# Spatial weights cast ahead of the last w_in quarter and of w_out, in an attention and gated-MLP kernel

## The chip, the cores and the metric

One NeuronCore of a Trainium2 chip. The metric is device time in microseconds (us) of one execution. Runs are timed beside runs of the kernel before on the same chip; a run over 1.5% above the fastest of its kernel is called slow and left out. A ratio in this document is the mean time of one kernel's fast runs over the mean of the other's fast runs of the same rounds, so it is not quite the ratio of the medians that stand beside it.

## The reference

Attention with grouped heads (8 batches, 16 query heads on 4 key heads, 384 positions, head size 64), whose output goes through a gated MLP with a mix over positions:

```
x     = attention(q, k, v)                    # [8, 384, 1024]
h     = max(x @ w_in, 0); u, v = halves of h  # w_in 1024 x 1024
v_n   = layernorm(v)
v_s   = w_spatial @ v_n + b_spatial           # 384 x 384, over positions
out   = (u * v_s) @ w_out                     # w_out 512 x 1024
```

Inputs and output are f32; the kernel computes in f16 with f32 sums.

## The kernel before

Work is written as words in strings, played in order; the program of each engine holds its own words in that order. `s`, `e`, `x`, `V`, `p`, `U`, `O` are scores, exponentials, values, and the MLP's parts; a plus means the next batch. The words that matter:

```python
# lk lq lv: load k, q, v of a batch on SP;  ck cq cv: cast them on GpSimd
# tk tq:    transpose k, q by DMA on SP
# wv wu:    load a quarter of w_in with a cast during the DMA, issued by GpSimd
# wo:       the same for w_out;  ws: load spatial weights and bias on SP
# cws: three casts of the spatial weights and a copy of the bias, on GpSimd
# tws: transpose them by DMA, issued by SP
RAMP1 = """
    ...
    cv wu0 lk+ lq0+ lq1+ lv+ ws ck+ cq0+ wv1
    ...
    cq1+ wu1 cv+ wo cws
    m10 r10 s16 e16 H0 x100 n100 x101 n101 s17 e17 s0+ e0+
    H1 s1+ e1+ m11 r11 s2+ e2+ x110 n110 x111 n111 Q10+ tws"""
FIRST = """lk+ lq0+ lv+ lq1+          # batch 2's loads, behind tws on SP
    s3 e3 s4 e4 V0' S0' s5 e5 V1' S1' ck+ cq0+
    s6 e6 s7 e7 V2' S2' s8 e8 Q11 tk+ tq0+ cq1+ cv+
    ...
    s15 s16 s17 e15 e16 e17 p2' U2' p3' U3' a10 a11"""

def cast_ws(engine):
    for tt in range(NST):
        engine.tensor_copy(ws16[:, tt, :, :],
            ws32[:, tt, :].rearrange("p (s t) -> p t s", t=NST))
    engine.tensor_copy(bias_tp..., bias_raw...)      # cut
```

SP sends its DMAs in the order of its program (in the first trace of before `tws` from 34.39 us, k from 37.11, q from 38.19), so batch 2's loads wait for `tws`, and `tws` waits for `cws` (13.2 us there). Batch 2's first scores on PE need its k and q, loaded, cast on GpSimd and transposed by DMA.

The softmax here doesn't subtract the row's maximum and nothing guards it: scores larger than these inputs give would overflow.

## Time and profile before

| | |
|---|---|
| time, median of the 3 runs first given | 253.27 us (253.07 to 253.46) |
| the profiled run | 256.59 us, its span on the core 254.8 us |
| PE, VectorE, ScalarE, GpSimd busy | 94%, 73%, 68%, 22% |

A busy share is an average over the span. Here PE is nearly full from batch 2 on (busy 90% or more in each of the page's 40 slices from 57.3 us to the last but one).

### The profile page before, as it was taken

How to read it: one execution, taken by the hardware profiler on the slowest of the kernel's cores; microseconds unless marked ns; L12 is line 12 of the kernel's file. 1: busy time of each engine (PE TensorE's matmuls, PEld its weight loads, DVE VectorE, ACT ScalarE, POOL GpSimd, SP SyncE). 2: the span in 40 equal slices, each digit the busy share in tenths (PEclk: the TensorE clock that was granted, in tenths of full speed). 3: DMA queues.
4: the chain of work that ended last, by engine and by line, in shares of the span. 5: the costliest groups of instructions: out<-in, count | busy, mean ns of one | idle time of the engine just before them, and what ended most of it. 6: DMA issues, size and time to landing. Idle time of an engine off the chain costs nothing.

```text
span 254.8 us, 6122 instructions
## 1 busy us (share of the span) xinstructions
PE 240.1 (94%) x2544; PEld 118.0 (46%) x2544; DVE 186.4 (73%) x347; ACT 172.1 (68%) x229; POOL 56.4 (22%) x100
## 2 busy tenths in 40 slices
PE   7689988859999999999999999999999999999993
PEld 6234434424355534444355444454355444554671
DVE  2536389985897679776996769776987669777853
ACT  3997999859596778678686778677785877430100
POOL 1825940552604400071004400170000000000000
PEclk9999999999999999999999999999999999999998
DMA  6999999989999383977099444958090202110324
GB/s 195 245 252 320 142 154 227 272 136 300 208 266 305 127 120 101 284 217 178 0 229 303 157 91 122 315 164 171 8 229 0 85 0 102 68 64 21 142 105 168
DMA packets 57228, 41.98 MB, mean 165 GB/s; under 512 B 26352, under 2 KB 53360, under 8 KB 57200
## 3 DMA queue, kind: packets, MB, share of 16 engines
q1 hardware_dynamic: 53936, 38.12, 56.9%
q0 software_dynamic: 2848, 3.15, 8.3%
q8 instruction: 20, 0.33, 0.5%
q10 hardware_dynamic: 416, 0.33, 0.4%
q14 instruction: 8, 0.07, 0.1%
HBM read 25.95 MB, written 12.58 MB: 151 GB/s over the span
## 4 chain that ended last, share of the span: by engine, by line
PE 57%; DVE 15%; DMA 13%; POOL 5%; issue 4%; ACT 3%; SPq 2%
PE banks L121 43%; DMA q<-in_q_dram 10%; PE banks L337 7%; PE banks L315 7%; DVE xT L407 3%; DVE sT L350 3%; DVE osb L545 3%; DVE v_n L481 3%; ACT aT L327 2%; POOL q L238 2%; POOL w_in L148 2%; DMA qT<-q 2%; DVE bn L467 1%; DVE v_r L454 1%; SPq L177 1%
## 5 line engine op out<-in xcount | busy, mean ns | idle before, releaser
L327 ACT ACTIVATE aT<-banks 128x1024 f16<-128x1024 f32 x144 | 136.6, 1025 | 38.2 <-PE banks L315 38.2
L315 PE MATMUL banks<-qT,kT 64*128 64x512 f16 x288 | 44.7, 380 | 6.8 <-DMA qT<-q 3.3
L121 PE MATMUL banks<-xT,w_in 128*128 128x384 f16 (+1 forms) x320 | 47.2, 294 | 0.8 <-DVE v_r L456 0.8
L121 PE MATMUL banks<-w_out,gT 128*32 128x512 f16 (+2 forms) x496 | 45.6, 378 | 0.0
L121 PE MATMUL banks<-w_in,xT 128*128 128x512 f16 x192 | 44.7, 380 | 0.1
L545 DVE COPY osb<-banks 128x512 f32<-128x512 f32 x46 | 30.4, 685 | 10.4 <-PE banks L121 10.4
L407 DVE TENSOR_TENSOR xT<-banks,rec 128x384 f16<-128x384 f32 x64 | 31.4, 550 | 8.9 <-ACT rec L376 8.8
L238 POOL CAST q<-q 128x384 f16<-128x384 f32 x57 | 30.5, 566 | 21.6 <-DMA q<-in_q_dram 19.9
L121 PEld LDWEIGHTS <-w_in 128*128 128x128 f16 x320 | 27.3, 98 | 16.2 <-issue 1.7
L337 PE MATMUL banks<-aT,v 128*32 128x384 f16 x768 | 34.4, 326 | 0.0
L121 PEld LDWEIGHTS <-gT 128*32 128x32 f16 (+1 forms) x496 | 18.7, 96 | 24.8 <-issue 6.4
L350 DVE TENSOR_TENSOR sT<-aT 128x1024 f16<-128x1024 f16 x39 | 30.1, 788 | 0.0
L121 PEld LDWEIGHTS <-xT 128*128 128x128 f16 x192 | 17.3, 98 | 25.4 <-issue 7.2
L195 POOL CAST k<-k 128x768 f16<-128x768 f32 x7 | 5.8, 829 | 93.0 <-DMA k<-in_k_dram 75.0
L315 PEld LDWEIGHTS <-kT 64*128 64x128 f16 x288 | 11.3, 94 | 31.5 <-issue 25.0
L337 PEld LDWEIGHTS <-v 128*32 128x32 f16 x768 | 20.6, 97 | 11.0 <-issue 1.2
L454 DVE TENSOR_SCALAR v_r<-banks 128x512 f32<-128x512 f32 x21 | 14.5, 692 | 13.4 <-PE banks L121 12.6
L525 DVE SCALAR_TENSOR_TENSOR gT<-banks,vs 128x384 f16<-128x384 f32 x24 | 13.4, 558 | 12.7 <-PE banks L121 12.2
L374 ACT ACTIVATE rec<-banks 128x384 f32<-128x384 f32 x32 | 15.7, 491 | 9.0 <-PE banks L337 9.0
L121 PE MATMUL banks<-wsT,v_n 128*128 128x384 f16 x96 | 20.6, 326 | 0.6
L376 ACT ACTIVATE rec<-rec 128x384 f32<-128x384 f32 x32 | 16.8, 524 | 1.0
L467 DVE BATCH_NORM_STATS2 bn<-v_r 128x6 f32<-128x512 f32 x24 | 16.7, 695 | 0.8
(49 smaller groups left out, 139.3 us busy)
## 6 DMA issues: line engine op xcount, KB each, us to landing
q<-in_q_dram SPq DMA_DIRECT2D x31, 384.0 KB, 7.1
out_dram<-osb SPq DMA_DIRECT2D x22, 512.0 KB, 3.1
v<-in_v_dram SPq DMA_DIRECT2D x8, 384.0 KB, 6.8
k<-in_k_dram SPq DMA_DIRECT2D x7, 384.0 KB, 5.5
w_in<-in_moe_w_in_dram POOLq DMA_DIRECT2D x16, 128.0 KB, 5.8
w_out<-in_moe_w_out_dram POOLq DMA_DIRECT2D x2, 512.0 KB, 9.1
out_dram<-osb SPq DMA_DIRECT2D x3, 256.0 KB, 2.0
ws<-in_moe_w_spatial_dram SPq DMA_DIRECT2D x1, 576.0 KB, 9.4
```

What stands on the lines that cost most here:

```text
L121: nc.tensor.matmul(dst[c : c + cols], w[:, c : c + cols], m, start=(i == 0), stop=(i == n - 1))
L238: engine(T["q16", b, gp][:, 2 * qd : 2 * qd + 2, :, half, :], T["q32", b, gp][:, qd, 2 * half : 2 * half + 2, :].rearrange("p j (t d) -> p ...
L315: nc.tensor.matmul(banks[:, xs[half], :], T["kT", b][lo:hi, t, gp, :], rhs[lo:hi, c * 512 : (c + 1) * 512], start=True, stop=True,)
L327: nc.scalar.activation(T["aT", b, gp][:, t, :, c * 512 : (c + 1) * 512], banks[:, x : y + 1 : y - x, :], AF.Exp, scale=scale)
L337: nc.tensor.matmul(dst[32 * i : 32 * (i + 1), :], weights if len(weights.shape) == 2 else weights[:, half, :], a[:, half, j * S : (j + 1) ...
L350: engine.tensor_tensor(T["sT", b, gp][:, :, cs], aT[:, 0, :, cs], aT[:, 1, :, cs], ALU.add)
L374: nc.scalar.activation(rec, f32(x, S), AF.Ln)
L376: nc.scalar.activation(rec, rec, AF.Exp, scale=-1.0)
L407: nc.vector.tensor_tensor(T["xT", b][:, gp * 4 + quad * 2 + jj, :], f32(x, S), T["rec", b, gp, quad], ALU.mult)
L454: nc.vector.tensor_scalar(v_r, banks[:, x, :], 0.0, None, op0=ALU.max)
L467: nc.vector.bn_stats(bn, T["v_r", b, st])
L545: copy(osb[:, half * 512 : (half + 1) * 512], banks[:, x, :])
```

## The change

Its intent: let the spatial weights' casts go first on GpSimd, so that SP is let go earlier and batch 2's loads are issued earlier.

```diff
-        cq1+ wu1 cv+ wo cws
+        cq1+ cws wu1 cv+ wo
         m10 r10 s16 e16 H0 x100 n100 x101 n101 s17 e17 s0+ e0+
-        H1 s1+ e1+ m11 r11 s2+ e2+ x110 n110 x111 n111 Q10+ tws"""
+        tws H1 s1+ e1+ m11 r11 s2+ e2+ x110 n110 x111 n111 Q10+"""
```

## The prediction

> **What bounds the kernel now.** I read the busy shares first: PE is busy 94% of the span and VectorE 73%, so time can come only from a stretch in which PE stands still, or from the ends. The list of waits, cut to PE and to 0 to 70 us, has one wait of any size; the second line is from the same list for the SP queue.
>
> ```profile
> PE banks L315 <- DMA qT<-q: 3.3, 1, 3.3
> ...
> SPq L177 <- POOL bias_tp L171: 13.2, 1, 13.2
> ```
>
> All other waits of PE in that stretch are 1.8 us or less together. PE waits 3.3 us once, for a transposed q tile, and SP stood 13.2 us on the spatial weights' transpose, which needs GpSimd's casts. The chain of work that ended last, in order of time, joins the two:
>
> ```profile
> 28.09 2.10 POOL w_in L148 x4
> 30.20 0.68 POOL v L206
> 30.88 0.08 issue
> 30.96 1.42 POOL w_out L155 x2
> 32.38 1.98 POOL setup L168 x3
> 34.36 0.66 POOL bias_tp L171
> 35.02 2.04 SPq L177
> 37.06 0.05 issue
> 37.11 1.03 SPq L189
> 38.14 0.05 issue
> 38.19 1.02 SPq L216
> 39.21 0.04 issue
> 39.26 8.64 DMA q<-in_q_dram
> 47.90 0.05 issue
> 47.95 1.33 POOL q L238 x2
> 49.30 4.13 DMA qT<-q
> 53.43 0.14 issue
> 53.56 0.41 PE banks L315 x2
> ```
>
> To be seen: GpSimd issues the last w_in quarter and w_out, casts the spatial weights, SP transposes them, then issues k and q of batch 2; the second half of q lands 8.64 us after its issue, is cast, transposed, and PE starts batch 2 at 53.56. PE had finished its previous work at 50.27. After 53.56 the chain is nearly all PE and the DVE steps between, repeated per batch. So what happens here is passed on to the end about one for one, and the ceiling of the gain is 3.3 us, or 1.3% of 253.27 us.
>
> The 8.64 us need a reason. In the trace's DMA view for 30 to 34 us and for 42 to 46 us:
>
> ```profile
> q0 software_dynamic: 529, 0.49, 107.2%
> ...
> q1 hardware_dynamic: 1671, 1.22, 108.7%
> ```
>
> q0 carries the casting loads of w_in and w_out, q1 what SP issues. Both fill the 16 engines (over 100%, as packets overlap). From about 29 to 38 us q1 moves nothing, because SP waits, and q0 alone has the engines; from 42 us q1 alone has them. Issue is early or late, but the transfers that have to be done before q lands are the same.
>
> [...] with both queues full, from 16 to 19 us, q0 moved 109, 110 and 126 records of w_in in one microsecond each, and q1 138 to 158 of q or v; from 44 to 46 us, alone, q1 moved 416 to 427 a microsecond. So q1 falls to about a third beside q0. [...] Here one w_in issue takes 0.54 us and lands about 5 us after its start.
>
> **The change part by part.** Nothing is added or removed. The order of instructions is the same on PE, VectorE, ScalarE and SP; on GpSimd the three casts and the bias copy move from behind w_out to ahead of the w_in quarter. The moved line of the transpose changes no place in SP's order, as SP has nothing between its old and its new place. One wait is new: the load of v for batch 2 must now wait explicitly for the cast of batch 1's v, as the transpose's wait no longer covers it.
>
> *GpSimd.* The last q cast ends at 28.09. The spatial weights land at 28.92 and the bias at 29.37 (semaphore records), so the casts start at about 28.95, not 28.09. With 1.98 + 0.66 us they end at about 31.6, against 35.02: SP is let go 3.4 us earlier. The four w_in issues then run 31.6 to 33.75, 3.55 us later than now; the v cast 33.75 to 34.6 (needed by PE at 41.66); w_out 34.6 to 36.0.
>
> *SP.* Its transpose issues 31.6 to 33.65, k to 34.7, q to about 37. If a load took as long to land as now, q would land at 44.5 instead of 47.9 and the whole 3.3 us of PE would go: 250.0 us. That is surely the intent.
>
> *DMA engines.* Here I differ. The data records of the w_in half before (issued at 24.1 to 26.2) are used up by about 29.7 and ws and bias by 28.5. The next w_in record can now start 1.5 us (the delay that the earlier group shows) after 31.6, at 33.1, and the transpose's first record 3.4 us after its release (as now: 35.02 to 38.4), at 35.0. So for 29.7 to 33.1, 3.4 us, the engines have nothing to do, where now they run w_in. Against that the queues overlap better later. Work to be done before q of batch 2 is in, by the bytes read: w_in 1.05 MB, w_out 2.10 MB, k and q 1.18 MB, and the transpose, which alone took 1152 records at about 600 a microsecond, 1.9 us. Now its last q record starts at 45.9 (my count of records) and the landing is 2.0 us later. Rates read from records: w_in alone averages 111 to 140 records a microsecond (2 KB read each, 230 to 290 GB/s), w_out in its steady part 100 (4 KB, 410 GB/s), q alone 330 GB/s, and the mixed stretch at 16 to 19 us about 345 GB/s. After, as an estimate:
> 1. w_in alone from 33.1 to 35.0 moves 0.45 MB. The other 0.6 MB run beside the transpose: 1.8 us at 330 GB/s plus 1.9 us, to about 38.6. Fully overlapped it would be 37.
> 2. w_out with k and q, 3.28 MB: 9.5 us at 345 GB/s, 8.0 us at 410. As q1 gets a part of the engines, neither finishes much before the other, and q's last record falls at 45 (37 + 8.0) to 48.1 (38.6 + 9.5); the middle is 46.7.
> 3. Against 45.9 that is 0.9 us earlier to 2.2 us later, with 0.7 us later as the middle. Its cast (1.33 us) and transpose (4.13 us) follow as now, and v and the other half of q, also 1.18 MB in the same queue ahead of the transpose of q, move in the same sense.
>
> *Other needs.* wsT is needed by PE at 44.26 (landed 42.81); it should land at about 40 to 41. The w_in quarter is needed at 44.76; landed 35.0, now about 40 to 42. w_out is needed at 54.32 and lands at about 48. None should stop PE, but the margin of w_in drops from 10 us to 3 or 4.
>
> *Sum.* 253.27 + 0.7 is 254.0. I leave it at 253.9, for the chance that q1 is served better than I count.
>
> **The rivals.**
> First, the queue is let go and the loads land 3.4 us earlier: 250.0 us. For it: w_in moved 110 to 126 records a microsecond beside q, hardly less than alone, so the mixture may be nearly free. Against it: w_out's steady 410 GB/s is already the most that any stretch shows, and q must share with it. At most about 1 us is to be had if 410 GB/s hold throughout.
> Second, the new order starves something that PE needs. If q1 gets few turns, wsT lands after 44.26 or w_in after 44.76, PE stops there, and batch 2 starts later as well: 255.5 to 257 us. For it: at 11 us q1 moved only 15 records while q0 moved 131. Against it: at 40 us, transpose against w_out, q1 moved 372 records of 256 bytes beside 35 of q0.
> Third, all is hidden, as PE waits for the end of one work-conserving stream: 253.3 us within 0.4.
>
> **Range and chances.** The estimate's ends, -0.9 and +2.2 us, give 252.4 to 255.5; I stretch the lower end to 251.4 for part of the first rival. A gain over 2% would need 5.1 us, more than PE's whole wait: 0.01. A loss over 2% needs a second stall of PE of some 4 us: 0.02.
>
> **What would show it.** SP's wait on the bias copy falls from 13.2 to about 9.8 us; GpSimd's casts start near 28.95 and w_in's issues near 31.6; the DMA view shows nearly empty engines from 30 to 33 us; q0 and q1 are both busy from 35 to 46 us; the second half of q lands between 47 and 50 us; PE's wait for qT is 2.4 to 5.5 us. I am wrong if q lands near 44.5 and PE's wait is gone, for then the engines served SP's loads without holding them back; or if PE waits for wsT or w_in near 44 us.

## The result, and the profile after

The kernel became slower, by 0.3 to 1.1% in three calls (the second and third were on chips 4 and 2). All three changes are under 2%, and the second call's interval holds 1:

| call | before, median | after, median | ratio of fast runs, 95% interval |
|---|---|---|---|
| first | 253.65 | 256.95 | 1.0107 [1.0059, 1.0154] |
| second (after_again) | 254.34 | 255.23 | 1.0031 [0.9968, 1.0095] |
| third (after_b) | 254.41 | 256.36 | 1.0052 [1.0001, 1.0103] |

The intervals are wide because single runs of one kernel differ by 5 to 6.5 us in these calls, slow ones counted. Weighted by their widths, the three ratios give 1.007 within 0.003, as an estimate. The first median lies above my range (251.4 to 255.5): the direction was right, the size too small.

The profile taken with the first call fell in a slow run (259.31 us). I therefore read two later traces of the changed kernel, of fast runs (255.2 and 257.84 us), and for the kernel before a second one, of a run of 253.4 us. The chain of work of the changed kernel, run of 255.2 us (start, length, what):

```profile
26.08 2.02 POOL setup L168 x3
28.11 0.66 POOL bias_tp L171
28.76 0.74 SPq L177
29.50 0.05 issue
29.55 0.65 SPq L189
30.21 0.04 issue
30.25 0.54 SPq L216
30.79 0.04 issue
30.84 15.65 DMA q<-in_q_dram
46.48 0.05 issue
46.54 0.97 POOL q L238 x2
47.51 0.02 issue
47.52 4.45 DMA qT<-q
```

The w_in and w_out issues are gone from the chain, as intended, and q is issued at 30.84, where the chain shown before had 39.26. But the transfer takes 15.65 us where it took 8.64. It has grown by 7.0 us, against a head start of 8.4. The two traces start at different times, though. Beside the second trace of before, where q was issued at 35.91 and landed at 43.68, the changed kernel issues it 5.1 us earlier and lands it 2.8 us later.

PE's wait for the transposed q, from the list of waits: the changed kernel at 255.2 us, then the changed kernel at 257.84 us, then the kernel before at 253.4 us.

```profile
PE banks L315 <- DMA qT<-q: 2.4, 1, 2.4
```
```profile
PE banks L315 <- DMA qT<-q: 2.6, 1, 2.6
```
```profile
PE banks L315 <- DMA qT<-q: 0.4, 1, 0.4
```

The wait of 3.3 us, on which the prediction builds, is not usual for the kernel before. A third trace of it (254.11 us) shows no such wait at all.

Where do the microseconds of the transfer come from? The DMA view for 27 to 29 us, changed kernel at 255.2 us, then before at 253.4 us (DMA: busy tenths of the 16 engines in 40 slices; then packets, MB, share):

```profile
DMA  1312213123032121190110101101101011010000
...
q0 software_dynamic: 48, 0.04, 13.0%
```
```profile
DMA  9999397997999999999899999997996999959798
...
q0 software_dynamic: 367, 0.33, 110.7%
```

The engines stand nearly idle in the changed kernel, because GpSimd is casting and has not issued the last w_in quarter, and SP still waits. In before they are full. From 38 to 42 us, same kernels in the same order:

```profile
q0 software_dynamic: 334, 0.65, 85.7%
q1 hardware_dynamic: 340, 0.25, 25.2%
```
```profile
q1 hardware_dynamic: 1985, 1.19, 114.1%
q0 software_dynamic: 1, 0.00, 0.0%
```

Now w_out in q0 shares the engines with batch 2's loads in q1, with about as many packets of each, 334 and 340 in 4 us: q1 moves 340 packets, where it moved 1985. In before w_out is through by then.

There is a second loss. The windows view of the changed kernel at 257.84 us (length, busy of each engine with counts, PEclk, DMA share, GB/s):

```profile
51.00:54.00 3.00, 0.64 (x6) 0.25 (x6) 2.97 (x6) 0.21 (x1) 2.52 (x4) 1.00 0.80 175
54.00:57.00 3.00, 3.00 (x9) 1.03 (x8) 1.96 (x4) 2.65 (x3) 0.00 (x0) 0.51 0.61 113
```

Behind the wait PE's granted clock is 0.51, and PE finishes 9 matmuls in 3 us. The timeline of PE in the same run, then in the first trace of before:

```profile
53.37 0.82 PE L315 MATMUL banks<-qT,kT 64*128 64x512 f16 x6 [2.55 <-DMA qT<-q]
54.12 3.54 PE L121 MATMUL banks<-w_out,gT 128*128 128x512 f16 x8
```
```profile
54.32 1.90 PE L121 MATMUL banks<-w_out,gT 128*128 128x512 f16 x8
```

The same eight matmuls take 3.54 us instead of 1.90.

### The profile page after: what moved, and what is told of

Same layout as the page of the kernel before. It is cut to its first block, busy times and chain, and to the rows that moved or that the text cites.

```text
span 257.5 us, 6122 instructions
## 1 busy us (share of the span) xinstructions
PE 242.8 (94%) x2544; PEld 118.7 (46%) x2544; DVE 186.6 (72%) x347; ACT 172.3 (67%) x229; POOL 57.9 (22%) x100
## 4 chain that ended last, share of the span: by engine, by line
PE 57%; DMA 17%; DVE 15%; issue 4%; POOL 2%; ACT 2%; SPq 2%
PE banks L121 44%; DMA q<-in_q_dram 8%; PE banks L315 7%; PE banks L337 6%; DMA ws<-in_moe_w_spatial_dram 5%; DVE xT L407 3%; DVE sT L350 3%; DVE osb L545 3%; DVE v_n L481 3%; DMA k<-in_k_dram 2%; DMA qT<-q 2%; DVE bn L467 1%; DVE v_r L454 1%; ACT aT L327 1%; POOL setup L168 1%
## 5 line engine op out<-in xcount | busy, mean ns | idle before, releaser
L315 PE MATMUL banks<-qT,kT 64*128 64x512 f16 x288 | 45.6, 385 | 7.7 <-DMA qT<-q 4.1
L121 PE MATMUL banks<-w_out,gT 128*32 128x512 f16 (+2 forms) x496 | 47.2, 383 | 0.0
L121 PE MATMUL banks<-w_in,xT 128*128 128x512 f16 x192 | 44.7, 380 | 0.2
L238 POOL CAST q<-q 128x384 f16<-128x384 f32 x57 | 31.6, 587 | 26.7 <-DMA q<-in_q_dram 26.3
```

Source lines behind the costliest of these rows:

```text
L121: nc.tensor.matmul(dst[c : c + cols], w[:, c : c + cols], m, start=(i == 0), stop=(i == n - 1))
L238: engine(T["q16", b, gp][:, 2 * qd : 2 * qd + 2, :, half, :], T["q32", b, gp][:, qd, 2 * half : 2 * half + 2, :].rearrange("p j (t d) -> p ...
L315: nc.tensor.matmul(banks[:, xs[half], :], T["kT", b][lo:hi, t, gp, :], rhs[lo:hi, c * 512 : (c + 1) * 512], start=True, stop=True,)
```

## The experiments

The kernels of one call share a chip.

**after_again and after_b: the changed kernel, unmodified.** No edit.

> The changed kernel once more, for a trace of an undisturbed run and for a timing beside the other three. Theory A (PE's wait for the transposed q grew from 3.3 to about 4.1 us, and that is enough for the TensorE clock to be halved for two periods of 3.4 us right behind it, as the one trace of it shows): ratio to before 1.008 to 1.013, and a trace with a stretch of granted clock 0.5 from about 52 to 59 us; a run in which the clock stays at 1.0 there would be only 0.6 to 1.0 us over before. Rival B (the run profiled was slow for another reason, and the loss is the DMA engines' contention throughout): the same ratio, but traces at full clock that are slow as well.

> The changed kernel a third time, beside the next three. From its two traces so far (waits of 4.1 and 2.4 us for the transposed q) and before's second (0.4 us): wait 2 to 4 us, time 1.0 to 3 us over before (ratio 1.004 to 1.012), and in some runs a clock 0.5 for 3.4 or 6.8 us behind the wait[...].

Measured: the ratios in the table above. The ratio of after_again lies under the range that was expected, and its trace lacks the half clock expected from 52 to 59 us. Theory A's other case came: that run, at full clock, took 0.9 us more than before's median (254.34). The waits were 2.4 and 2.6 us. The trace of after_b has one period of half clock behind the wait (and one at 13.1 to 16.5 us, long before it), so the half clock comes in some runs only.

**before_again and before_c: the kernel before, unmodified.**

> The kernel before, unmodified, for a second trace of it. The first trace is of a run of 256.59 us, 3.3 us over the median of the timed runs (253.27). Theory D (that trace was of an unusually slow start, and most runs of before have a PE wait for the transposed q well under 3.3 us): the trace of a run at 253 to 254 us shows a wait of 0 to 1.5 us. Theory E (the wait of 3.3 us is in all its runs, and the 3.3 us of the profiled run are elsewhere): again about 3.3 us. Ratio to itself 1.000 within 0.004 either way.

> The kernel before for one more trace. Theory D (the usual wait of PE for the transposed q is short, the first trace was of a slow start): the time is 253 to 254.5 us and the wait 0 to 1.2 us; if the run takes 256 us or more, the wait is again 2 us or more. Theory E: 3 us or more at 253 us.

Measured: 253.88 us median, ratio to itself 0.9986 [0.9936, 1.0037]; the traces show waits of 0.4 and 0 us. Theory D holds. The first trace was of a run with a late start: its fourth w_in quarter was issued at 28.05, against 25.64 and 24.78 in these two.

**after_fill and after_fill10: keep PE busy in the gap.**

```diff
+    def fill(b, n):        # idle matmuls, no bank is taken
+        x = min((i for i in range(8) if not busy[i]), key=lambda i: used[i])
+        for _ in range(n):
+            nc.tensor.matmul(f32(x, P), warm, warm, start=True, stop=True)
-        ... p2' U2' p3' U3' a10 a11"""
+        ... p2' U2' p3' U3' z40 a10 a11"""      # z10 in the other
```

> The changed kernel with 40 idle matmuls on PE in the gap before batch 2's first scores, so that PE is busy for some 3 us of its wait of 4.1 us. It moves no data and PE waits for the same transpose. Theory A: the clock stays at 1.0 and the time falls by 2.0 to 2.6 us against the changed kernel, to 0.5 to 1.1 us over before (ratio 1.002 to 1.004). Rival B (the transfers alone make the loss): ratio stays at 1.010 to 1.011. Rival C (idle matmuls delay the scores): slower than the changed kernel.

> The same with only 10 idle matmuls, some 0.7 to 0.8 us, at the start of the gap. [...] the clock stays and the time is that of the 40 matmuls within 0.3 us. If it is the length of unbroken idleness that counts, it is also shortened, to 3.3 us, the length that before has without a drop[...]. If nothing but a full gap filled helps, the time stays at a ratio of 1.010.

Measured: 257.17 us (ratio 1.0089) and 257.19 us (1.0046). Neither gained: after_again took 255.23 us. In the trace with 40 the clock stays at 1.0, but PE still starts only at 53.09. The idle matmuls did not hold it up (rival C), as it waited another 0.82 us behind them. PE started right behind the last of the 16 semaphore marks of the transposed q: fifteen came by 51.55 us, the last at 53.05. At 51.00 a transfer of 16 KB had begun in the queue of kind "instruction"; it took 0.99 us. With 10 the same: 52.53, 54.05, and a 16 KB transfer at 51.99. In the three traces of the unfilled changed kernel it came at 54.4 to 55.5; that the added matmuls moved it is a guess of mine, not shown. With 10 the clock was halved behind the wait all the same (54.69 to 58.11), against what was expected. As times, these two kernels settle nothing about the clock.

**after_fillw: the same with fewer matmuls.** Four f32 matmuls of 384 columns in place of the 40, in the hope that the 16 KB transfer then comes when it does in the unfilled changed kernel.

```diff
-            nc.tensor.matmul(f32(x, P), warm, warm, start=True, stop=True)
+            nc.tensor.matmul(f32(x, S), ident, ws32[:, 0, :], start=True, stop=True)
```

> The changed kernel with four f32 matmuls of 384 columns in the gap, in place of the 40 of 128 columns[...]. Theory A (half clock behind the wait is part of the changed kernel's loss): no half clock at 50 to 60 us, the last of the 16 DMA engines' marks of the transposed q comes with the others, time 0.5 to 1.7 us under the changed kernel of the same call. Rival (half clock there is rare or costs nothing): equal to the changed kernel within 0.4 us.

Measured: 256.88 us (ratio 1.0088 [1.0058, 1.0119]) beside the changed kernel's 256.36, so no gain. The hope failed: the 16 KB transfer came at 51.75 us, and the last mark at 53.81, 1.5 us behind the fifteenth. In after_again and mid_b one of 0.9 us lay on the second transpose of q, whose last mark came 1.6 us late, against 0.25 in before_again. I saw the transfer and the late mark together and did not test the link. The clock stayed at 1.0 behind the wait, as theory A has it. Filling the gap is left inconclusive as to time.

**before_gap and before_gap5: lengthen the wait in the kernel before, move no transfer.**

```diff
+    def cast_q_late(b, gp):
+        cast_q(b, gp, pool, 0, 0)
+        cast_q(b, gp, pool, 1, 0)
+        cast_q(b, gp, pool, 0, 1)
+        for _ in range(1):           # 5 in before_gap5
+            nc.gpsimd.tensor_copy(scratch, ws32[:, 0, :])
+        cast_q(b, gp, pool, 1, 1)
-        ... V1' S1' ck+ cq0+
+        ... V1' S1' ck+ cqz0+
```

> The kernel before with one extra copy of 0.66 us on GpSimd ahead of the last cast of batch 2's first q, which makes PE's wait about 4.0 us without touching the order of the weights' casts or of any transfer. Theory A: the clock halves after the gap and the time rises by 2.5 to 3.2 us (0.7 us of gap and some 2.2 us of clock), ratio 1.009 to 1.013, as in the changed kernel. Rival B (the loss comes of the moved transfers): only the 0.7 us of the gap are lost, ratio 1.002 to 1.004.

> The kernel before with five extra copies of 0.66 us on GpSimd ahead of the last cast of batch 2's first q, 3.3 us in all, so that PE waits some 3.3 to 4.3 us for the transposed q. Theory A[...]: the trace shows half clock of 3.4 or 6.8 us behind the wait, and the stretch from the first spatial matmul of batch 1 to that of batch 2 is 28.3 us plus the wait plus 1.4 us (one period) or 2.3 us (two). Median time 3.5 to 6 us over before (ratio 1.014 to 1.023). Rival B: full clock, only the 3 to 3.7 us of the wait, and the stretch is 28.3 us plus the wait.

Measured: before_gap 254.15 us, ratio 0.997 [0.9903, 1.0037], wait 1.0 us and full clock behind it. It rested on the wait of 3.3 us that is not there, so it could not show what it was for. before_gap5 was made for the wait as it is: median 257.93 us beside 254.47. Two of its six runs are slow (259.46 and 259.42 us, granted clock 0.987), and the ratio of the rest is 1.0053 [0.9985, 1.0122], below what I expected and not clear of noise. Its trace decides the question of the clock. PE's timeline:

```profile
53.77 1.46 PE L325 MATMUL banks<-qT,kT 64*128 64x512 f16 x6 [3.69 <-DMA qT<-q]
55.16 2.82 PE L121 MATMUL banks<-w_out,gT 128*128 128x512 f16 x8
```

With all loads where they were, a wait of 3.69 us was followed by half clock for 3.4 us (records of the granted clock: 53.64 to 57.05). So a wait is enough for it, without the change's moved transfers. It is one trace.

**before_hole: a hole, and everything behind it later.** Copies on GpSimd in the place to which the change moved the casts, while the casts stay last and SP is let go later, not earlier.

```diff
-        cq1+ wu1 cv+ wo cws
+        cq1+ y4 wu1 cv+ wo cws      # y4: four copies of 128x384
```

> The kernel before with four copies of 0.66 us on GpSimd (2.65 us) ahead of the last w_in quarter, in the place to which the change moved the spatial weights' casts, which here stay last. SP is let go 2.65 us later than in before, not earlier. Theory F'' (the DMA engines are the bound from about 25 to 48 us, and a hole of 2.65 us in what they are given delays the q of batch 2 by about as much): q lands 2 to 2.7 us later than before's 43.7, PE waits 2 to 3.1 us, as in the changed kernel; ratio 1.005 to 1.014. Rival (the engines have slack and the hole is made up for): wait under 1 us, ratio under 1.003.

Measured: 257.37 us beside 254.47, ratio 1.0124 [1.0074, 1.0174]. The four copies took 2.22 us. A delay at this place costs time, and the rival's ratio (under 1.003) fell. The trace fell on the fastest of its runs (254.54 us): q landed at 45.85, against 43.68 in before_again, and PE waited 1.7 us. But the run does not single out the hole, since the copies delay all that stands behind them on GpSimd, and so SP's release. There q was issued at 37.07 and took 8.78 us, about as in before (8.64 and 7.77). Nor is its landing beyond what before's order gives by itself: 41.8 to 47.9 us in the three traces of before, and 46.14 in before_gap, which has no hole.

**mid and mid_b: half of the change.** The casts ahead of w_out, but behind the w_in quarter.

```diff
-        cq1+ wu1 cv+ wo cws
+        cq1+ wu1 cws cv+ wo
```

> Half of the change: the spatial weights' casts ahead of w_out, but behind the last w_in quarter. This keeps the DMA engines fed at 28 to 30 us, and lets SP go about 1.4 us earlier than before; w_out is issued 2.7 us later and runs beside batch 2's loads. If the hole costs the changed kernel its time (Rival G), this gains: ratio 0.993 to 0.998. If w_out beside the loads costs it (Theory F), q lands no earlier than in before within 1 us, ratio 0.999 to 1.006.

> The half change (casts behind the last w_in quarter, ahead of w_out) once more, beside the changed kernel. If the w_in quarter moved behind the casts is what costs the changed kernel its time: PE does not wait for the transposed q (under 0.4 us), the time is 1 to 3 us under the changed kernel's of the same call and within 0.4% of before (ratio 0.997 to 1.001). If not: within 0.4% of the changed kernel.

Measured: 254.18 us beside 254.14 (0.9991 [0.9939, 1.0042]) and 254.37 beside 254.41 (0.9989 [0.9958, 1.0019]). In that call it is 1.4 us under the changed kernel by the means of fast runs, which is not clear of noise; both calls weighted as above give 0.999 within 0.003, against 1.007 for the change, and that is. In the first trace w_out shares the engines with q (80 packets of each per us from 38 to 40 us), yet q lands at 42.95 and PE does not wait. The DMA view of that stretch:

```profile
q0 software_dynamic: 161, 0.33, 86.5%
q1 hardware_dynamic: 161, 0.12, 24.7%
```

In the second, a late start, it waits 1.7 us, where under 0.4 was expected. So w_out beside the loads does not by itself make q late; what the change loses comes with the w_in quarter behind the casts.

**early_wo: w_out into the hole.**

```diff
-        cq1+ cws wu1 cv+ wo
+        cq1+ wo cws wu1 cv+
```

> The change with w_out issued ahead of the casts instead of last. The DMA engines then have w_out to do at 26 to 32 us, and batch 2's loads run beside the w_in quarter, whose records are half as long as w_out's. Theory F' (hole plus sharing with w_out, whose records take 0.16 us each, made q late): q lands at 39 to 43 us, PE's wait for its transpose is 0 to 0.3 us, ratio to before 0.996 to 1.001. Rival H (whatever is put ahead of the loads in q0, q lands at the same time): q lands at 46 us or later, wait over 2 us, ratio 1.004 or more.

Measured: 256.12 us, ratio 1.0048 [1.0011, 1.0085]; its profile fell in a slow run. I had expected q by 43 us; it landed at 47.82 and PE waited 3.5 us. Theory F' failed, and rival H's numbers came. The engines had w_out to do in place of the hole (their share was over 100% from 28 to 33 us), and q was as late: the loss needs no hole. What this kernel shares with the changed one is the w_in quarter behind the casts. The DMA view of 34 to 38 us of that run has a possible reason that I had not thought of:

```profile
q1 hardware_dynamic: 365, 0.09, 101.3%
q0 software_dynamic: 106, 0.11, 45.0%
```

The spatial transpose in q1 moved 365 packets of 256 bytes in 4 us beside the casting load of w_in, taking 178 ns each on average, where it took 23 ns in the idle hole of the changed kernel. I saw this stretch in one trace, of a slow run, and did not repeat it; that it makes up the whole loss of this kernel stays open.

**after_late_wo and before_late_wo: w_out behind the cast of batch 2's k.**

```diff
-        cq1+ cws wu1 cv+ wo         # before_late_wo: cq1+ wu1 cv+ wo cws
+        cq1+ cws wu1 cv+            #                 cq1+ wu1 cv+ cws
-        ... V1' S1' ck+ cq0+
+        ... V1' S1' ck+ wo cq0+
```

> The changed kernel with the two w_out loads issued behind the cast of batch 2's k instead of ahead of it, so that batch 2's loads do not share the DMA engines with w_out. Theory F (in the changed kernel, the loads of batch 2 go one record for one beside w_out's records, of 4 KB read each, some 85 a microsecond against 430 alone, from about 38 to 44 us): q of batch 2 lands 3 to 5 us earlier than in the changed kernel, at 41 to 44 us, PE does not wait for the transposed q (under 0.5 us), and the time is 1.5 to 3 us under the changed kernel, ratio to before 0.990 to 1.000. Rival G (the order of w_out does not matter, what matters is the hole in the DMA engines' work at 28 to 30 us): q lands as in the changed kernel, ratio 1.003 to 1.011. A risk in both: w_out lands after 52 us and PE waits for it instead.

> The kernel before with only w_out moved behind the cast of batch 2's k; the weights' casts stay behind the last w_in quarter. The DMA engines have no hole at 28 to 30 us, and w_out is out of the way. Theory F: q of batch 2 lands at 40 to 43 us, PE does not wait for its transpose, ratio to before 0.985 to 0.998. Rival: w_out now starts late and holds back the rest of batch 2's loads or PE's first use of w_out, ratio 1.000 or more.

Measured: 257.2 us (1.0072 [1.0008, 1.0136]) and 254.4 us (1.0023 [0.9962, 1.0083]). Half of theory F came true: q landed at 41.87 and 38.56, 4.6 and 5.1 us earlier than with w_out ahead. But its transpose landed at 52.67 and 51.51, and PE waited 2.9 and 0.9 us. w_out then ran beside the transposes (466 packets of q0 beside 748 of q1 from 43 to 49 us in after_late_wo), and kT, issued from 40.57 in after_late_wo, landed at 51.3. The delay went from the load to the transpose.

**What the traces say together.** From the first spatial matmul of batch 1 to that of batch 2, PE has a fixed piece of work, the wait, and whatever the clock costs. I took that stretch in each trace without fillers:

| kernel | stretch | wait | periods at half clock | stretch less wait |
|---|---|---|---|---|
| before, first trace | 31.55 | 3.29 | 0 | 28.26 |
| before_again | 28.90 | 0.40 | 0 | 28.50 |
| before_c | 28.63 | 0 | 0 | 28.63 |
| before_gap | 29.28 | 1.02 | 0 | 28.26 |
| before_late_wo | 29.17 | 0.92 | 0 | 28.25 |
| before_hole | 29.96 | 1.70 | 0 | 28.26 |
| mid_b | 30.00 | 1.74 | 0 | 28.26 |
| mid | 28.33 | 0 | 0 | 28.33 |
| after_again | 30.64 | 2.39 | 0 | 28.25 |
| after_b | 32.30 | 2.55 | 1 | 29.75 |
| after_late_wo | 32.63 | 2.89 | 1 | 29.74 |
| before_gap5 | 33.34 | 3.69 | 1 | 29.65 |
| early_wo (slow run) | 34.13 | 3.48 | 2 | 30.65 |
| after, first trace (slow run) | 34.51 | 4.08 | 2 | 30.43 |

Without half clock the rest is 28.25 to 28.63 us in every kernel. Against 28.3 us, one period adds 1.4 to 1.5 us and two add 2.2 to 2.4. (A period is a half-clock record of 3.4 us, as that in before_gap5; the record of 6.83 us in the first trace of after counts as two.) The length of the wait alone does not decide: 2.55 us in after_b was followed by half clock, 3.29 us in the first trace of before was not. Behind that stretch the traces run alike, with 179.0 to 179.1 us to the end in all fourteen. Ahead of it lie 43.8 to 44.7 us in before and 43.7 to 44.8 in after. So in these traces the wait and the clock are the whole of what the change did to PE.

The granted clock of single runs tells more than the traces. In the traces a mean of 0.991 to 0.993 went with one halved period (0.991 in before_gap5, 0.993 in before_c) and 0.985 to 0.987 with two (after, after_b, early_wo); so, as an estimate, I take a mean under 0.99 for two periods or more. Of the 52 runs of before with a clock on record none is under 0.99; of the 18 of the changed kernel five are (0.980 to 0.987), and they took 257.4 to 260.5 us. In the second and third calls the changed kernel's five runs at 0.999 or 1.0 average 255.0 us, and before's eleven fast runs at 0.996 or more 254.2. Two things limit this. A mean near 0.992 is, by the same estimate, one period, which need not lie behind the wait: before_c, before_gap and after_b have one at about 13 to 16.5 us. And the rule that calls a run slow at 1.5% over the fastest leaves out just such runs, two each of before_gap5 and before_hole at 0.985 to 0.987 (the four slow runs of before are at 0.991 to 0.993), so the ratios of fast runs can understate the loss.

## Why the prediction was right or wrong

*Order of instructions: right.* SP's order did not change, and GpSimd's did as I had it. SP's wait on the bias copy fell from 13.3 us in before_again to 9.3 in after_again. The casts, and behind them the w_in quarter, also had to wait for the load of the spatial weights: 2.39, 0.85 and 1.39 us in the three traces of after, where I had 0.86.

*The hole in the DMA engines: there, but not shown to be the cause.* I had 3.4 us of idle engines from 29.7 on; after_again has it from about 27 to 29.4, and a second, smaller one at 32 us. mid and mid_b show that the order of casts and w_in quarter costs the time. Whether it is the hole or the later w_in and w_out beside batch 2's loads stays open: before_hole delays SP as well, and early_wo is as late without the hole. My reading that q0 filled the engines from 30 to 34 us was too strong, too. Its 107.2% is a sum of overlapping packets, and in the same view 16 of 40 slices stand at 6 tenths or less.

*"As an estimate ... the middle is 46.7", 0.7 us later: mis-sized.* The traces start at different times, so I count from the issue of the third w_in quarter, which the change does not touch, to the landing of the transposed q. It is 29.3, 28.3 and 28.9 us in the three traces of before, and 31.8, 30.7 and 31.0 in the three of after. The means, 28.9 and 31.2, differ by 2.3 us: the term was 0.7 and measured 2.3, just over the upper end of 2.2 that I gave it. (The landing of q itself, counted so, moved from 22.2 to 25.7; its cast and transpose made up a part.) Of the 1.6 us missing about 0.5 is the first trace, whose own 29.3 was the latest of its three. That I credited the later stretch with a better overlap of the queues than it had is a guess for the rest. The middle of 45 and 48.1 is 46.55, not 46.7, which changes little.

*"What happens here is passed on to the end about one for one": the step that failed.* It left out the clock. A longer wait is not only added to the end; in two of the three traces of after PE's clock was also halved behind it for one or two periods, which cost 1.5 and 2.2 us. Beside those traces stands before_gap5, where a longer wait alone brought it, for 1.4 us. Between the two first traces the wait grew by 0.8 us, nearly my 0.7, and the clock took 2.2 us more.

*"The ceiling of the gain is 3.3 us": wrong.* It was read from a trace of 256.59 us beside runs of 253.27, and that difference was on the page. In runs near the median PE hardly waits (0.4 and 0 us), so there was hardly anything to win. That the wait came out in the first trace of after (3.3 plus 0.7 is 4.0, and it was 4.1), and in or at the edge of my range of 2.4 to 5.5 us in all three, was in part luck: the wait started from too high and grew by more than I had.

*The rivals.* The first (all loads 3.4 us earlier) fell. The second (PE starved for wsT or w_in at 44 us) fell: wsT landed at 32.4 in after_again, w_in at 38.3. That its 255.5 to 257 us holds the first median is luck. The third (all hidden) fell.

*Sum.* With hindsight, an estimate for a run with the usual wait would have been some 2 us of transfers, plus 1.4 to 2.4 us of clock in some runs. The means of fast runs were 0.3 to 1.1% higher, 0.8 to 2.7 us. I can't give the share of the clock in the mean exactly: the runs at full clock were 0.8 us over before's, those with two halved periods or more over 3 us.

What stays open: why runs of one kernel start up to 3.3 us apart (the issue of the fourth w_in quarter in before), what in the w_in quarter's later place makes q late, and whether mid is faster than before. Its two ratios lie under 1, but both intervals hold 1, so no kernel here is shown to beat before.

## What to carry to other kernels

Here an issue 5.1 us earlier gave nothing, as the w_in quarter was held back for it; look first at what a move stops issuing meanwhile. A PE wait of 2.5 to 4.1 us could cost more than its length here, as half clock came behind it in five of six traces of unfilled kernels, for 1.4 to 2.4 us. Before building on a wait, check that the profiled run took as long as the timed ones.
